# A parametric rectifier on ScalarE carries the sign of the weights through their narrowing, in a kernel of gated recurrent attention and two MLPs on one core

## The chip, the cores and the metric

One core of a Trainium2 chip runs one program. The metric is the time of the program on the device in microseconds; the kernel before has a median of 514.72 us over three runs (514.72, 515.02 and 509.17).

## The reference

Three stages follow one another. The first is a recurrence with gates over 768 steps, for 2 batches and 8 heads of 40 features; the other two are MLPs over the 1,536 resulting tokens of 320 features.

```python
# recurrence, for each batch and head
m_new = maximum(f[t] + m, i[t])
C = exp(f[t] + m - m_new) * C + exp(i[t] - m_new) * outer(v[t], k[t])
n = exp(f[t] + m - m_new) * n + exp(i[t] - m_new) * k[t]
y[t] = sigmoid(o[t]) * (C @ q[t]) / max(abs(n @ q[t]), 1)
# first MLP: w_a, w_b 320 x 1536, w_out 1536 x 320
x = (x @ w_a) * (x @ w_b) @ w_out
# second MLP: w_in 320 x 2048, w_out 2048 x 320
h = x @ w_in
out = (h * sigmoid(h)) @ w_out
```

The weights of both MLPs arrive as 64-bit floats, everything else as 32-bit floats. The products are formed to about 24 bits.

## The kernel before, in words

**Work and tiles.** The recurrence is cut into chunks of 128 tokens. A unit is one chunk of all heads of one batch; the two batches take turns, so there are 12 units. For each unit VectorE scans the decay factors into a matrix (`decays`, L329), TensorE forms scores (L349), VectorE weighs them (`weigh`, L356), TensorE forms values (L362) and the carried state (L372, L382), and VectorE, ScalarE and GpSimd combine the outputs (L418 to L436). `x_transposed` (L448) turns a unit's output by features into a ring `xring` for the first MLP. ScalarE's sigmoid of a unit's output gate is L413.

The MLPs are cut into tiles of 128 hidden features: 12 tiles for the first and 16 for the second. For each tile and each block of two or three units, `first_layer` (L473) forms the hidden products, ScalarE and VectorE form the gate (L506 and L512, or L517 for the second MLP), `split_g` (L486) splits it into a high part (ScalarE, L488) and a rest (GpSimd, L197), and `second_layer` (L482 to L484) adds it into the output.

**Preparation of the weights.** Each weight tile is loaded as 64-bit numbers, seen as pairs of 32-bit words (`raw_j`, L173 and L179, queue of SyncE). `narrowed` (L185) makes 32-bit floats of them, with one ScalarE and three VectorE instructions: ScalarE scales the high word, read as a float, by 2^-111, which moves its exponent field (L188); VectorE shifts the result left by three bits, which puts the exponent and the mantissa where a 32-bit float has them and pushes the sign out (L189); VectorE adds the top three bits of the low word (L190); VectorE adds the sign bit of the high word (L192). ScalarE then rounds the tile to a high part (L206, L214, L217 for the first MLP; L225, L228 for the second) and GpSimd forms the rest (`rest`, L197). A tile of the first MLP is narrowed in two parts, of 448 and 512 columns; a tile of the second in one, of 704 columns. That makes 24 and 16 calls. The parts of the first MLP are loaded into 4 buffers in turn, those of the second into 3; the narrowed tiles lie in 2 buffers each (`cvt`, `cvt2`), which come free when GpSimd has formed the last rest.

**Order.** The list `ORDER` (L31) names the parts of the work up to the last pass of the first MLP; the program is written in that order. A planner (`schedule_with_timeline_sim`, L709) then sets the order of the instructions on each engine: it plays the program with modelled costs and issues what is ready, earlier parts first. So the order on an engine may differ from the list, and it is fixed once the program is built. On each engine instructions then run in that order, and one that waits holds back all behind it. The preparation of the second MLP's tiles (`prep2`, L615) is issued from the last pass of the first MLP on (`block`, L622). 150 small products (`warm`, L296) run on TensorE near the start while it has little else to do.

Of the kernel before, what the change touches and what calls it, by code (L numbers as in the profile page):

```python
# [8 lines left out]
F32 = mybir.dt.float32  # L9
# [3 lines left out]

# The first MLP's passes: a block of tokens and the tiles of the hidden features. The first blocks take
# two passes each, so that the weights' preparation spreads over more products.
PASSES = ((0, range(0, 5)),
# [10 lines left out]

# The order in which the parts of the work are issued up to the last pass of the first MLP, by name:
# l<unit>.* loads of a unit, u<unit>.* its steps, lw<j> and w<j>.* loads and preparation of a weight tile,
# m<pass>.<j>.* products of a pass; those marked ! go ahead of all others that are ready.  # L30
ORDER = """  # L31
# [31 lines left out]

# Parts that wait for the end of another on VectorE.
AFTER = {'w1.a': 'u1.out', 'w1.b': 'u1.out', 'u4.d0': 'u3.w1'}

ACT = mybir.ActivationFunctionType
ALU = mybir.AluOpType
# [3 lines left out]
def tile_mlstm_gated_mlps(ctx: ExitStack, tc: tile.TileContext, i_gate, f_gate, q_cols, k_cols, kvo, w1, w2,  # L72
                          out):
    nc = tc.nc
    B, S, _, H, D = kvo.shape
    BH = B * H
    DM = H * D
    P = 128
    C = 128                      # tokens of a chunk of the recurrence
    NC = S // C  # L80
    NT = B * NC                  # units: a chunk of all heads of a batch; the batches take turns
    DV = D + 1                   # values and the normalizer's column
    G = 3                        # heads of a group; the groups are heads 0-2, 3-5, 5-7
    GR = G * D
    GH = (0, 3, 5)
    SLOT = {h: (h // G, h % G) if h < 6 else (2, h - 5) for h in range(H)}
    BLOCKS = {1: (2, 2, 2, 3, 3), 2: (3, 3, 3, 3)}     # units of each block of the MLPs
    TB = 3 * P
    UNITS, AT = {}, {}
    for m, sizes in BLOCKS.items():  # L90
        for blk, n in enumerate(sizes):
            lo = sum(sizes[:blk])
# [3 lines left out]
    J1, J2 = w1.shape[0], w2.shape[0]  # L96
    KT = DM - 2 * P              # rows of the last tile of the contraction over features
    WN = 10 * P + 2 * DM
    EARLY = 4                    # first units, while the MLPs need little PSUM
    BUSY = 6                     # first units, while VectorE prepares weights  # L100
    WARM = 150                   # matmuls that only keep the clock up
    WS = 2.0 ** 8                # scale of the weights on chip
    NEG = -1e30
    PSUM = bass.MemoryType.PSUM
# [18 lines left out]
    idb = const.tile([P, P], BF16, name="idb")  # L123
    ident8 = cat.tile([P, H, C], F32, name="ident8")
    mask = cat.tile([P, G], F32, name="mask")
    bmask = cat.tile([P, G, G, DV], F32, name="bmask")
    isg = cat.tile([P, NC, 2, BH], F32, name="isg")
    gb = cat.tile([GR, B * G, NC], F32, name="gb")
    fsd = dram.tile([BH, S], F32, name="fsd")
    x1 = {u: const.tile([P, 3 * P], F32, name=f"x1_{u}") for u in range(NT) if AT[1, u][0] < NB1 - 1}  # L130

    def place(u):
        c, b = divmod(u, B)
        return b, c, slice(c * C, (c + 1) * C)

# [1 line left out]
    un = {}  # L137

    def load_q(u):
        b, c, s = place(u)  # L140
        t = at.tile([GR, G, C], F32, tag="qT", name=f"qT_u{u}")
        nc.sync.dma_start(out=t, in_=q_cols[b, c])
        un["q", u] = t

    # Each head's keys by rows of its group, among zeros.
    kz = [cat.tile([GR, G, G, C], F32, name=f"kz{i}") for i in range(2)]

# [12 lines left out]
    def load_fs(u):  # L160
        b, c, s = place(u)
        t = at.tile([P, H, C], F32, tag="e", name=f"e_u{u}")
        nc.sync.dma_start(out=t, in_=fsd[b * H:(b + 1) * H, s].partition_broadcast(P))
# [17 lines left out]

# [1 line left out]
    W = {}  # L183

    def narrowed(r, c):  # L185
        lo32, hi32 = r[:, :, 0], r[:, :, 1]
        cu = c.bitcast(U32)
        nc.scalar.activation(out=c, in_=hi32.bitcast(F32), func=ACT.Copy, scale=2.0 ** -111)  # L188
        nc.vector.tensor_scalar(out=cu, in0=cu, scalar1=3, scalar2=None, op0=ALU.logical_shift_left)  # L189
        nc.vector.scalar_tensor_tensor(out=cu, in0=lo32, scalar=29, in1=cu,  # L190
                                       op0=ALU.logical_shift_right, op1=ALU.bitwise_or)
        nc.vector.scalar_tensor_tensor(out=cu, in0=hi32, scalar=0x80000000, in1=cu,  # L192
                                       op0=ALU.bitwise_and, op1=ALU.bitwise_or)
        return c
# [3 lines left out]

    # First layers: hi hi hi hi [hi_a; lo_a] [lo_b; hi_b] lo lo lo lo; then w_out's hi and lo.
    def split_w1(j, part):  # L200
# [18 lines left out]

    # First layer: hi hi [hi; lo] lo lo; then w_out's hi and lo.  # L220
    def split_w2(j, pool, tag, bufs):
# [9 lines left out]

# [1 line left out]
    scratch = [wp.tile([P, WN], F32, tag="w", name="scratch", bufs=J1) for _ in range(2)]  # L233
# [60 lines left out]

    # Keeps TensorE's clock up while it waits.
    def warm(n):  # L296
# [4 lines left out]

# [1 line left out]
    state = {}  # L303

    def chunk(u):
# [26 lines left out]
        def scale_v():  # L332
            T["v"] = vx = at.tile([P, H, DV], F32, tag="vx", name=f"vx_u{u}")
            nc.gpsimd.tensor_copy(out=vx[:, :, D:DV], in_=isb.unsqueeze(2))
            nc.gpsimd.tensor_tensor(out=vx[:, :, 0:D], in0=un["v", u],
# [22 lines left out]
        def values(n):  # L358
            if n == 0:
                T["y1"] = ps_at.tile([P, H, DV], F32, tag="at", name=f"y1_u{u}")  # L360
            for h in range(4 * n, 4 * n + 4):
# [82 lines left out]

    # A block's tokens by features: hi hi [hi; hi] lo lo [lo; lo]
    px = {}
# [10 lines left out]

# [1 line left out]
    # Slot of the weights, slot of the tokens.  # L459
    PAIRS = {  # L460
# [30 lines left out]

    # The parts of an MLP's work on a block, for the tiles js of the hidden features.
    def mlp(m, blk, js):
# [45 lines left out]

# [1 line left out]
    ch = [chunk(u) for u in range(NT)]  # L541
    run0, expf0, expi0 = gates(0, C)
    run1, expf1, expi1 = gates(C, S)
    passes = [mlp(1, blk, js) for blk, js in PASSES]
# [31 lines left out]
    def load_i():  # L576
        nc.sync.dma_start(out=ig, in_=i_gate.rearrange("b h s -> (b h) s"))

    parts = {"lf": load_f, "li": load_i, "const": constants, "bmask": masks, "zeros": zeros, "sel": selectors,
             "warm": lambda: warm(WARM), "run0": run0, "expf0": expf0, "expi0": expi0, "run1": run1,  # L580
             "expf1": expf1, "expi1": expi1, "starts": gate_starts, "prod": gate_products,
             "pg0": lambda: gate_columns(True), "pg1": lambda: gate_columns(False)}
    for u in range(NT):
        parts.update({f"u{u}.{n}": f for n, f in ch[u].items()})
# [129 lines left out]
```

## Time and profile before

| | |
|---|---|
| Median of three runs | 514.72 us |
| All runs | 514.72, 515.02, 509.17 us |
| Profiled execution: span | 509.0 us (its time outside the span is not shown) |
| TensorE busy | 474.2 us, 93% |
| VectorE busy | 234.7 us, 46% |
| ScalarE busy | 209.9 us, 41% |
| GpSimd busy | 272.7 us, 54% |
| Mean granted TensorE clock | 0.982 |

The span goes from the first to the last instruction of one profiled execution. The shares are averages over stages that differ: VectorE has nearly all of its work in the first 140 us and between 240 and 340 us. In the profile PE is TensorE's products, PEld its weight loads, DVE VectorE, ACT ScalarE, POOL GpSimd and SPq the queue of loads. A group of instructions is shown with its line, engine, operation, tiles and shape, then the count, busy time, mean time of one in ns, and the idle time ahead of them with what ended it.

### The profile page before, as it was taken

To read this page: it belongs to the slowest core of one execution; us is meant where nothing else is said; L and a number is where in the kernel's file an instruction comes from. 1 tells how busy PE (TensorE), PEld (TensorE's weight loads), DVE (VectorE), ACT (ScalarE), POOL (GpSimd) and SP (SyncE) were. 2 spreads that over 40 slices of the span, in tenths; PEclk is the share of its full clock that TensorE was granted. 3 is DMA by queue.
4 is the path that set the end of the run, shared out by engine and by line. 5 is a ranking of instruction groups with operands and counts; after the bars stand their busy time and mean duration, and the time that the engine had idled before them with its cause. 6 is when DMAs were issued, how large, how long until landed. Compare 5 with 4: busy or idle time off the path is not lost.

```text
span 509.0 us, 8482 instructions
## 1 busy us (share of the span) xinstructions
PE 474.2 (93%) x3261; PEld 460.6 (90%) x3261; DVE 234.7 (46%) x368; ACT 209.9 (41%) x479; POOL 272.7 (54%) x305
## 2 busy tenths in 40 slices
PE   7898788897799999999989998999999999999996
PEld 6798778786699999999989987899999999999996
DVE  7999999889934254543674667710010010000000
ACT  4255545544322322222444453663353344334332
POOL 5548987987942241323583788773333433334333
PEclk9988998999989999999999999999999999999999
DMA  7666657636310012104342153100010001001001
GB/s 230 214 196 208 196 174 196 200 123 193 92 57 1 0 54 72 40 1 160 124 135 94 57 169 117 58 1 1 1 39 1 1 0 40 2 0 40 0 1 39
DMA packets 25091, 42.33 MB, mean 83 GB/s; under 512 B 2156, under 2 KB 18348, under 8 KB 25052
## 3 DMA queue, kind: packets, MB, share of 16 engines
q1 hardware_dynamic: 25052, 41.80, 25.9%
q8 instruction: 25, 0.41, 0.3%
q14 instruction: 14, 0.11, 0.1%
HBM read 38.99 MB, written 2.02 MB: 81 GB/s over the span
## 4 chain that ended last, share of the span: by engine, by line
PE 58%; DVE 15%; POOL 14%; ACT 5%; issue 4%; DMA 3%; SPq 0%; ACTq 0%; DVEq 0%; POOLq 0%
PE h L473 31%; POOL w_j L197 9%; PE acc L482 7%; PE acc L483 7%; PE acc L484 7%; DVE e_u L329 4%; DVE cvt_j L190 3%; DVE cvt_j L192 2%; DMA e_u<-fsd 2%; ACT cvt_j L188 2%; PE s_u L349 2%; DVE cvt_j L189 2%; POOL tl_j L197 2%; PE y_u L362 2%; POOL g L197 1%
## 5 line engine op out<-in xcount | busy, mean ns | idle before, releaser
L473 PE MATMUL h<-xring,w_j 128*128 128x384 f32 (+1 forms) x1472 | 264.7, 321 | 8.8 <-DVE g L512 7.3
L473 PEld LDWEIGHTS h<-xring,w_j 128*128 128x128 f32 x1472 | 230.2, 190 | 14.8 <-DVE g L512 11.7
L197 POOL TENSOR_TENSOR g<-g,g 128x384 fp32r<-128x384 f32 (+1 forms) x124 | 121.5, 980 | 180.5 <-ACT g L488 178.7
L482 PE MATMUL acc<-w_j,g 128*128 128x320 f32 x336 | 102.8, 315 | 1.6 <-ACT g L488 1.5
L483 PE MATMUL acc<-w_j,g 128*128 128x320 f32 x336 | 101.4, 310 | 0.0
L488 ACT CAST g<-g 128x384 fp32r<-128x384 f32 (+1 forms) x124 | 59.7, 482 | 98.5 <-DVE g L512 60.0
L197 POOL TENSOR_TENSOR w_j<-cvt_j,w_j 128x320 fp32r<-128x320 f32 (+2 forms) x72 | 79.5, 1104 | 9.8 <-ACT w_j L225 5.0
L484 PE MATMUL acc<-w_j,g 128*128 128x320 f32 x336 | 77.2, 315 | 1.6 <-POOL g L197 1.6
L482 PEld LDWEIGHTS acc<-w_j,g 128*128 128x128 f32 x336 | 63.7, 190 | 3.5 <-ACT g L488 3.4
L483 PEld LDWEIGHTS acc<-w_j,g 128*128 128x128 f32 x336 | 63.8, 190 | 0.0
L484 PEld LDWEIGHTS acc<-w_j,g 128*128 128x128 f32 x336 | 56.8, 189 | 2.7 <-POOL g L197 2.6
L517 ACT ACTIVATE g<-h 128x384 f32<-128x384 f32 x64 | 31.6, 493 | 60.0 <-PE h L473 53.5
L512 DVE TENSOR_TENSOR g<-a,h 128x256 f32<-128x256 f32 (+1 forms) x60 | 27.9, 466 | 49.8 <-PE h L473 49.5
L197 DVE TENSOR_TENSOR xring<-px_u,xring 128x384 fp32r<-128x384 f32 x24 | 12.4, 548 | 83.2 <-PE h L473 80.5
L190 DVE SCALAR_TENSOR_TENSOR cvt_j<-raw_j,cvt_j 128x704 uint32<-128x704 uint32 (+2 forms) x40 | 46.8, 1173 | 0.9
L188 ACT ACTIVATE cvt_j<-raw_j 128x704 f32<-128x704 f32 (+2 forms) x40 | 28.9, 726 | 39.5 <-POOL w_j L197 37.4
L192 DVE SCALAR_TENSOR_TENSOR cvt_j<-raw_j,cvt_j 128x704 uint32<-128x704 uint32 (+2 forms) x40 | 39.4, 986 | 0.6
L506 ACT ACTIVATE a<-h 128x256 f32<-128x256 f32 (+1 forms) x60 | 25.5, 424 | 32.9 <-PE h L473 32.7
L189 DVE TENSOR_SCALAR cvt_j<-cvt_j 128x704 uint32<-128x704 uint32 (+2 forms) x40 | 22.5, 565 | 23.7 <-ACT cvt_j L188 23.7
L349 PE MATMUL s_u<-qT_u,kz 120*128 120x128 f32 x192 | 28.8, 289 | 3.1 <-ACT a L506 2.3
L349 PEld LDWEIGHTS s_u<-qT_u,kz 120*128 120x128 f32 x192 | 25.2, 198 | 3.9 <-ACT a L506 2.5
L362 PE MATMUL y_u<-vx_u,e_u 128*128 128x41 f32 x192 | 26.5, 280 | 2.2 <-DVE e_u L356 2.2
(84 smaller groups left out, 379.0 us busy)
## 6 DMA issues: line engine op xcount, KB each, us to landing
raw_j<-in_w_dram SPq DMA_DIRECT2D x16, 704.0 KB
raw_j<-in_w_dram SPq DMA_DIRECT2D x12, 512.0 KB
kvo_u<-in_kvo_dram SPq DMA_DIRECT2D x12, 480.0 KB
raw_j<-in_w_dram SPq DMA_DIRECT2D x12, 448.0 KB
e_u<-fsd SPq DMA_DIRECT2D x10, 512.0 KB
qT_u<-in_q_cols_dram SPq DMA_DIRECT2D x12, 180.0 KB
kz<-in_k_cols_dram SPq DMA_DIRECT2D x36, 60.0 KB
out_dram<-osb SPq DMA_DIRECT2D x12, 160.0 KB
```

The costliest lines, as they stand in the source:

```text
L188: nc.scalar.activation(out=c, in_=hi32.bitcast(F32), func=ACT.Copy, scale=2.0 ** -111)
L189: nc.vector.tensor_scalar(out=cu, in0=cu, scalar1=3, scalar2=None, op0=ALU.logical_shift_left)
L190: nc.vector.scalar_tensor_tensor(out=cu, in0=lo32, scalar=29, in1=cu, op0=ALU.logical_shift_right, op1=ALU.bitwise_or)
L192: nc.vector.scalar_tensor_tensor(out=cu, in0=hi32, scalar=0x80000000, in1=cu, op0=ALU.bitwise_and, op1=ALU.bitwise_or)
L197: return eng.tensor_tensor(out=out_, in0=x, in1=hi.bitcast(F32), op=ALU.subtract)
L349: nc.tensor.matmul(out=s[:, i], lhsT=kz[u % 2][:, j, g], rhs=un["q", u][:, g], start=True, stop=True)
L362: nc.tensor.matmul(out=T["y1"][:, h], lhsT=un["e", u][:, h], rhs=T["v"][:, h], start=True, stop=True)
L473: nc.tensor.matmul(out=po, lhsT=w[:, wi * P:(wi + 1) * P], rhs=xt[:, :, xi], start=(n == 0), stop=(n == len(pairs) - 1))
L482: nc.tensor.matmul(out=o, lhsT=hi, rhs=w[:, off:off + DM], start=first, stop=False)
L483: nc.tensor.matmul(out=o, lhsT=hi, rhs=w[:, off + DM:off + 2 * DM], start=False, stop=False)
L484: nc.tensor.matmul(out=o, lhsT=lo, rhs=w[:, off:off + DM], start=False, stop=last)
L488: nc.scalar.copy(out=t[:, 0], in_=g)
```

## The change

In `narrowed` the scaling on ScalarE uses the function Prelu in place of Copy: for an input that is not negative the result is the input times 2^-111 as before; for a negative one it is that times alpha, -2^32, so a positive number whose exponent field is higher by 32. The shift by three bits puts that bit of the exponent where the sign belongs. The third VectorE step, which took the sign from the high word, is dropped. The only other edits are comments that are taken out (blank lines stand for most of them; not shown).

```diff
     def narrowed(r, c):
         lo32, hi32 = r[:, :, 0], r[:, :, 1]
         cu = c.bitcast(U32)
-        nc.scalar.activation(out=c, in_=hi32.bitcast(F32), func=ACT.Copy, scale=2.0 ** -111)
+
+        nc.scalar.activation(out=c, in_=hi32.bitcast(F32), func=ACT.Prelu, scale=2.0 ** -111, alpha=-2.0 ** 32)
         nc.vector.tensor_scalar(out=cu, in0=cu, scalar1=3, scalar2=None, op0=ALU.logical_shift_left)
         nc.vector.scalar_tensor_tensor(out=cu, in0=lo32, scalar=29, in1=cu,
                                        op0=ALU.logical_shift_right, op1=ALU.bitwise_or)
-        nc.vector.scalar_tensor_tensor(out=cu, in0=hi32, scalar=0x80000000, in1=cu,
-                                       op0=ALU.bitwise_and, op1=ALU.bitwise_or)
         return c
```

## Rows read from the trace of the kernel before

**Rows 1.** Stretches: busy us (and instructions) per engine, granted clock, DMA.
```profile
core 0: us, PE busy (x) PEld busy (x) DVE busy (x) ACT busy (x) POOL busy (x), PEclk, DMA share, GB/s
0.00:140.00 140.00, 115.35 (x924) 108.30 (x925) 128.43 (x193) 65.94 (x164) 107.26 (x133) 0.95 0.60 184
140.00:240.00 100.00, 99.62 (x750) 99.38 (x750) 41.67 (x97) 26.18 (x64) 32.34 (x42) 0.99 0.14 42
240.00:340.00 100.00, 94.22 (x555) 88.26 (x554) 61.65 (x74) 52.17 (x113) 71.02 (x70) 1.00 0.30 103
340.00:509.00 169.00, 164.98 (x1039) 164.68 (x1037) 2.97 (x6) 65.59 (x139) 62.03 (x61) 1.00 0.04 13
```

**Rows 2.** VectorE by line and shape: count, busy us, mean ns.
```profile
L192 DVE SCALAR_TENSOR_TENSOR cvt_j<-raw_j,cvt_j 128x704 uint32<-128x704 uint32 x16 | 18.5, 1159 | 0.5
...
L190 DVE SCALAR_TENSOR_TENSOR cvt_j<-raw_j,cvt_j 128x512 uint32<-128x512 uint32 x12 | 12.2, 1015 | 0.2
...
L192 DVE SCALAR_TENSOR_TENSOR cvt_j<-raw_j,cvt_j 128x512 uint32<-128x512 uint32 x12 | 10.5, 878 | 0.0
...
L192 DVE SCALAR_TENSOR_TENSOR cvt_j<-raw_j,cvt_j 128x448 uint32<-128x448 uint32 x12 | 10.3, 861 | 0.1
...
L189 DVE TENSOR_SCALAR cvt_j<-cvt_j 128x512 uint32<-128x512 uint32 x12 | 6.5, 539 | 2.1 <-ACT cvt_j L188 2.1
```

**Rows 3.** Chain of waits, first 140 us: share by line.
```profile
by line: DVE e_u L329 14.1%; DVE cvt_j L190 9.4%; DVE cvt_j L192 7.4%; issue 7.3%; POOL tl_j L197 5.7%; POOL w_j L197 5.7%; DVE cvt_j L189 5.4%; DMA e_u<-fsd 4.3%; PE h L473 4.1%; DVE x_u L433 2.9%; ACT cvt_j L188 2.7%; DVE e_u L356 2.4%; D
```

**Rows 4.** Waits, first 140 us: total, times, longest.
```profile
ACT w_j L214 <- DVE cvt_j L192: 21.3, 11, 4.6
...
ACT w_j L206 <- DVE cvt_j L192: 12.4, 6, 3.7
```

**Rows 5.** Waits of the load queue, whole span.
```profile
SPq L173 <- DVE cvt_j L192: 35.7, 16, 5.1
```

**Rows 6.** GpSimd, one form: first 140 us, then 140 to 240.
```profile
L197 POOL TENSOR_TENSOR g<-g,g 128x256 fp32r<-128x256 f32 x14 | 15.0, 1074 | 1.7 <-ACT g L488 1.7
...
L197 POOL TENSOR_TENSOR g<-g,g 128x256 fp32r<-128x256 f32 x22 | 16.2, 738 | 40.2 <-ACT g L488 40.2
```

**Rows 7.** Chain of waits, 240 to 340 us.
```profile
by line: POOL w_j L197 40.3%; PE h L473 16.0%; issue 8.1%; POOL g L197 6.1%; ACT cvt_j L188 5.8%; ACT w_j L225 4.5%; ACT g L488 3.4%; PE acc L482 2.8%; PE acc L484 2.6%; PE acc L483 2.5%; PE px_u L452 1.6%; DVE cvt_j L192 1.6%; ACT L517 1.3
```

**Rows 8.** Timeline, two tiles of that stretch: start, us, idle before.
```profile
297.73 0.85 ACT L188 ACTIVATE cvt_j<-raw_j 128x704 f32<-128x704 f32 x1 [2.65 <-POOL w_j L197]
...
298.48 0.50 ACT L488 CAST g<-g 128x384 fp32r<-128x384 f32 x1
...
299.06 1.02 POOL L197 TENSOR_TENSOR g<-g,g 128x384 fp32r<-128x384 f32 x1 [1.36 <-ACT g L488]
...
300.03 3.40 POOL L197 TENSOR_TENSOR w_j<-cvt_j,w_j 128x256 fp32r<-128x256 f32 x3
...
300.85 1.31 DVE L192 SCALAR_TENSOR_TENSOR cvt_j<-raw_j,cvt_j 128x704 uint32<-128x704 uint32 x1
...
302.09 0.54 DVE L512 TENSOR_TENSOR g<-a,h 128x384 f32<-128x384 f32 x1
...
308.11 0.84 ACT L188 ACTIVATE cvt_j<-raw_j 128x704 f32<-128x704 f32 x1 [2.64 <-POOL w_j L197]
```

**Rows 9.** ScalarE by line and shape.
```profile
L188 ACT ACTIVATE cvt_j<-raw_j 128x704 f32<-128x704 f32 x16 | 13.6, 847 | 23.1 <-POOL w_j L197 23.1
...
L228 ACT CAST w_j<-cvt_j 128x320 fp32r<-128x320 f32 x16 | 7.3, 459 | 0.0
...
L413 ACT ACTIVATE kvo_u<-kvo_u 128x320 f32<-128x320 f32 x12 | 5.5, 466 | 3.3 <-DMA kvo_u<-in_kvo_dram 3.3
...
L413 ACT ACT_TABLE_LOAD x1 | 1.3, 1283 | 0.0
```

**Rows 10.** ScalarE timeline, 0 to 140 us: first, last of eight sigmoid groups.
```profile
11.69 0.83 ACT L413 ACTIVATE kvo_u<-kvo_u 128x320 f32<-128x320 f32 x2
...
138.26 0.47 ACT L413 ACTIVATE kvo_u<-kvo_u 128x320 f32<-128x320 f32 x1
```

## The prediction

> **What bounds the kernel now.** I read the stretches first, because shares over the whole span mix stages [rows 1]. In the first 140 us VectorE is busy for 128.4 us (92%) and TensorE for 115.4, of which some belongs to products that only fill time; GpSimd has 107.3, ScalarE 65.9. So VectorE is the fullest engine there, and TensorE is idle for 24.6 us. From 140 to 240 us TensorE is busy for 99.6 of 100: nothing else matters. From 240 to 340 us it is idle for 5.8 us, and it also does fewer instructions than it could (555 in 100 us; the last stretch has 1039 in 169 us, which is 615 in 100): about 60 instructions, or 10 us, are lost. After 340 us TensorE alone sets the pace and VectorE has 3 us of work. The change touches VectorE and ScalarE, so it can move the end only through the first and the third stretch. In both, what they finish earlier passes on to the end, since TensorE is full behind them.
>
> The chain of waits of the first 140 us comes next [rows 3]: the dropped line L192 has 7.4% of it, 10.4 us. The waits say who is held up by it: ScalarE's rounding of a narrowed tile waits on L192 for 21.3 and 12.4 us there [rows 4]. Then the third stretch: in its chain GpSimd's rests have 40.3%, L192 1.6% [rows 7].
>
> **The sum, part by part.**
>
> *The dropped step, first stretch.* Of the 24 calls for the first MLP, 12 have 448 columns at 861 ns and 12 have 512 at 878 ns [rows 2]: 10.3 + 10.5 = 20.8 us leave VectorE's 128.4. From above, the gain is all 20.8 us: VectorE would stay as full as it is and the stretch would end that much earlier. From below it is nothing, if another engine takes over at once. Between them stands the chain's share, 10.4 us [rows 3]. I take 10.4: VectorE at 108 of 130 us would then be 83% full, and the 24.6 us in which TensorE is idle [rows 1] have room for it, while a gain of 20.8 would ask TensorE to work in 119 us with hardly an idle moment, although each unit's steps wait for each other.
>
> *What it gives to GpSimd.* One form, the rest of the gate at 128x256, takes 1074 ns in the first 140 us and 738 ns in the next stretch, where VectorE is 42% busy [rows 6]: 46% more beside a full VectorE. GpSimd's rests on the chain are 5.7 + 5.7% [rows 3], 16 us; of their 46%, some 5 us lie in the chain as slowing, and L192 is 16% of VectorE's busy time (20.8 of 128.4) but more of what reads two tensors. I take 1.4 us, with ends 0 and 5.
>
> *The dropped step, third stretch.* 16 x 1159 ns = 18.5 us leave VectorE [rows 2]. The loop that sets the pace is another one [rows 8]: ScalarE's L188 waits for GpSimd's rest to free a buffer, L488 stands behind it in ScalarE's order, GpSimd idles 1.36 us for L488, then forms the gate's rest (1.02) and three weight rests (3.40). VectorE's steps run beside these 3.40 us. L192 only delays VectorE's L512 behind it (302.09), and so a L488 whose result GpSimd could not take before 303.4 anyway. So I cost it at nothing, with GpSimd's rests as the cover. If the cover is gone (a new order in which L488 goes ahead of L188 each time), about 1 us of that idle goes for each of some six pairs of tiles: 6 us, the upper end. The lower end is 0.
>
> *Prelu for Copy.* The trace has no Prelu. Its nearest rows say that ScalarE's time goes by size and hardly by function: a sigmoid of 128x320 takes 466 ns and a rounding copy of that size 459 [rows 9]. So L188 stays at 847 ns for 704 columns. Bounds: nothing from below, since the instruction reads and writes the same; from above a second pass, another 847 ns.
>
> *The load queue.* No load is added or moved, but L192 was the last reader of a raw buffer. The loads L173 wait on it for 35.7 us in all [rows 5], and what is queued behind them (units' inputs, the scans' factors) waits too. With L190 as the last reader each buffer comes free some 0.9 us earlier (861 and 878 ns). I add nothing: weights that come earlier also compete with the units' loads, and the loads are not the bound.
>
> Sum: 10.4 + 1.4 = 11.8 us. The profiled execution has a span of 509.0 us; what lies around it is not shown, and the fastest of the three runs, 509.17, stands as close to it as a run can. Its own time less the sum is 497.2 us. The median of the runs is 5.7 us longer than the span; taken from it, the same sum gives 514.7 - 11.8 = **502.9 us**, 2.3% less. That is the forecast, **503 us**.
>
> **A rule that bears on the second term.** The row above shows GpSimd slower beside a full VectorE, with no cause in it [rows 6]. The Trainium skill's GPSIMD Engine Reference, section Key points, says that GpSimd shares its SBUF interfaces with VectorE and contends with VectorE instructions that have two SBUF inputs, which L192 has. By that rule most of the slowing, not a share of it, would come from steps like L190 and L192, and the sum would be near 15 us and not 11.8.
>
> **The rivals.**
>
> *All of it counts* (0.15). VectorE is the bound of the first stretch throughout, so 20.8 us go: 493.9. For it speaks 92% busy; against it that the chain runs on VectorE for about half of its length only.
>
> *The next queue takes over* (0.25). GpSimd at 107.3 us and the units' own chain bind as soon as VectorE eases. Then only the part of TensorE's idle time goes that is L192's share of VectorE's work: 16% of 24.6 = 3.9 us, 510.8. For it speaks that GpSimd's rests are on the chain too [rows 3].
>
> *Prelu costs more than Copy* (0.03). L188 stands in the third stretch's loop: about 12 of its 16 tiles x 0.85 us = 10.2 us there, against 11.8 gained: 513.1.
>
> *Prelu needs another function table* (0.04). The trace loads a table three times, 1283 ns each [rows 9]. Ten sigmoids stand in eight groups between narrowings in the first 140 us [rows 10]; if the two functions did not share a table, 1 + 6 x 2 + 1 loads would come there and one before the third stretch: 15 x 1.283 = 19.2 us on ScalarE, which has 74 us of idle time in that stretch. All on the path would give 522.1; half of it 512.5. The Trainium skill's page ScalarE: Activation LUTs, section Table sets, names relu, copy, identity and abs as functions that every table has, and not the parametric rectifier; with the drain that the page adds to a load (2.66 us in all, an estimate from that page: 40 us) the time would be 543. No run so far shows a Prelu or that drain.
>
> *Slower: the planner's new order* (0.08). With cheaper narrowings the planner may put them ahead of the units' steps on VectorE. Each narrowing put ahead holds a unit back by L189 and L190, 0.54 + 1.02 = 1.56 us for 512 columns [rows 2]. Eight units are scanned from stored factors in that stretch; two narrowings ahead of each cost 8 x 3.1 = 25 us, and TensorE waits for the units' outputs: 514.7 - 11.8 + 25 = 528. It decides from some 22 us on, 14 narrowings put ahead; below that the result stays within 2%. Against it: the list is unchanged, and the units' parts stand early in it.
>
> **Numbers.** The forecast has 0.45, with a range of its own of 499 to 507. I take 2% for what a measurement can tell from no change: below 504.4 or above 525.0. Faster is three quarters of the forecast's chance and all of the first rival: 0.49. Slower is the last rival and a part of the table's: 0.10. The rest, 0.41, is within 2%. The range goes from the first rival, 494, up to 514, where the next queue has taken all; outside lie the slower cases and a gain that adds the third stretch's 6 us to 20.8.
>
> **What would show it.** VectorE's busy time falls by 39 us in all. Right: VectorE's full stretch ends near 128 us, not 140, TensorE's idle time ahead of it falls by about as much, and the third stretch keeps its pace of 10.4 us for two tiles (297.73 to 308.11 [rows 8]). L188 at 847 ns and three table loads show Prelu to be free; more loads show the table's rival. If the first stretch is as long as before with VectorE near 80%, the next queue has it; if L329 or L356 come later than before, the order has changed. A third stretch that is shorter by more than 2 us means that the cover was not what I took it for.

## The result and the profile after

The changed kernel takes 494.21 us (median of four runs, 493.73 to 496.84); the kernel before, beside it on the same chip, 514.29 us (509.17 to 515.02). The ratio is 0.9651 [0.9594, 0.9708]: **faster by 3.5%**. The profiled execution took 493.73 us with a span of 491.8, against the 509.0 of before: 17.2 us of the difference can be followed in the two traces.

In the changed file the narrowing is Prelu L189, shift L190, low word L191; every later line has a number smaller by one (L512 is L511, GpSimd's rest L197 is L196). The stretches after, with the columns of [rows 1] (busy us and instructions of TensorE, its weight loads, VectorE, ScalarE, GpSimd; granted clock; DMA):

```profile
core 0: us, PE busy (x) PEld busy (x) DVE busy (x) ACT busy (x) POOL busy (x), PEclk, DMA share, GB/s
0.00:140.00 140.00, 123.04 (x995) 118.54 (x996) 113.76 (x174) 69.21 (x175) 108.95 (x140) 0.94 0.61 185
140.00:240.00 100.00, 100.00 (x750) 99.90 (x749) 44.64 (x98) 29.00 (x65) 32.27 (x41) 1.00 0.19 58
240.00:340.00 100.00, 98.09 (x592) 95.14 (x591) 38.45 (x50) 53.12 (x115) 65.25 (x71) 1.00 0.25 85
340.00:491.80 151.80, 147.54 (x930) 147.24 (x928) 2.97 (x6) 59.30 (x125) 55.00 (x55) 1.00 0.04 14
```

Against [rows 1]: in the first 140 us VectorE falls from 128.4 to 113.8 us and TensorE rises from 115.4 to 123.0, at much the same granted clock (0.94 after 0.95). GpSimd does 140 instructions there and not 133, in 109.0 us. In the third stretch TensorE rises from 94.2 to 98.1 us and from 555 to 592 instructions. So both stretches gained, and the prediction had given the third nothing.

Fixed windows cut different work, so I set two landmarks on ScalarE: its first narrowing of a 704-column tile (the second MLP's weights begin) and its last table load (they are done). Start, duration, engine, line; the kernel before and then the changed one:

```profile
243.29 0.83 ACT L188 ACTIVATE cvt_j<-raw_j 128x704 f32<-128x704 f32 x1
...
330.88 1.28 ACT L517 ACT_TABLE_LOAD   x1
```

```profile
232.26 0.83 ACT L189 ACTIVATE cvt_j<-raw_j 128x704 f32<-128x704 f32 x1
...
313.20 1.28 ACT L516 ACT_TABLE_LOAD   x1
```

Up to the first landmark 243.29 - 232.26 = 11.0 us are gained. Between the two it is 87.59 before and 80.94 after, another 6.65. From the second to the end it is 178.1 and 178.6, a loss of 0.5. These add up to the 17.2 us.

VectorE's lines after (count, busy us, mean ns, idle before):

```profile
L191 DVE SCALAR_TENSOR_TENSOR cvt_j<-raw_j,cvt_j 128x704 uint32<-128x704 uint32 x16 | 21.9, 1370 | 0.5
...
L190 DVE TENSOR_SCALAR cvt_j<-cvt_j 128x704 uint32<-128x704 uint32 x16 | 9.9, 618 | 23.5 <-ACT cvt_j L189 23.5
```

The step L192 is gone with its 39.4 us (16 + 12 + 12 calls). VectorE's busy time on the page falls from 234.7 to 199.8, by 34.9 only, because neighbouring records overlap a little: the lines add up to 251.4 us before and 212.8 after, and some of that overlap goes with the step. The 704-column shift L190 takes 618 ns a call, where it took 524; the low word's step beside it takes 1370 for 1429, so the two together change little.

The chain of waits of the first 130 us after, by line:

```profile
by line: PE h L472 11.7%; issue 8.3%; DVE e_u L328 6.3%; DMA raw_j<-in_w_dram 5.8%; PE s_u L348 5.7%; DVE cvt_j L191 4.7%; DVE cvt_j L190 4.2%; DMA e_u<-fsd 3.9%; POOL tl_j L196 3.5%; POOL w_j L196 3.3%; PE y_u L361 2.7%; DMA fsd<-scratch 2
```

In [rows 3] the narrowing's three VectorE lines had 22.2% of 140 us; its two now have 8.9% of 130. TensorE's L472, the first layer's products, leads the chain with 11.7%. ScalarE's rows:

```profile
L189 ACT ACTIVATE cvt_j<-raw_j 128x704 f32<-128x704 f32 x16 | 13.6, 849 | 16.6 <-POOL w_j L196 16.6
...
L516 ACT ACT_TABLE_LOAD x1 | 1.3, 1283 | 0.0
```

Prelu takes 849 ns where Copy took 847 [rows 9], and loads of a table at the narrowings there are none: the program still has three. The loop of the third stretch, two tiles of it (start, us, idle before and its releaser):

```profile
297.03 0.84 ACT L189 ACTIVATE cvt_j<-raw_j 128x704 f32<-128x704 f32 x1 [2.12 <-POOL w_j L196]
...
298.34 1.02 POOL L196 TENSOR_TENSOR g<-g,g 128x384 fp32r<-128x384 f32 x1 [1.35 <-ACT g L487]
...
299.31 2.88 POOL L196 TENSOR_TENSOR w_j<-cvt_j,w_j 128x256 fp32r<-128x256 f32 x3
...
303.57 2.75 POOL L196 TENSOR_TENSOR w_j<-cvt_j,w_j 128x256 fp32r<-128x256 f32 x3 [0.39 <-ACT w_j L224]
...
306.36 0.83 ACT L189 ACTIVATE cvt_j<-raw_j 128x704 f32<-128x704 f32 x1 [2.12 <-POOL w_j L196]
```

Two tiles take 306.36 - 297.03 = 9.33 us; in [rows 8] it is 10.38. The order is the same, and GpSimd's two idle gaps too, 1.35 and 0.39 us. What has shrunk is GpSimd's own work: the three weight rests take 2.88 and 2.75 us in place of 3.40 and 3.28. By form (count, busy us, mean ns), before (250 to 330 us) and then after (235 to 313 us), the parts between the landmarks where the rests run:

```profile
L197 POOL TENSOR_TENSOR w_j<-cvt_j,w_j 128x320 fp32r<-128x320 f32 x14 | 15.9, 1135 | 1.1
L197 POOL TENSOR_TENSOR w_j<-cvt_j,w_j 64x128 fp32r<-64x128 f32 x14 | 13.3, 952 | 1.1
L197 POOL TENSOR_TENSOR w_j<-cvt_j,w_j 128x256 fp32r<-128x256 f32 x13 | 12.8, 988 | 3.6 <-ACT w_j L225 3.6
```

```profile
L196 POOL TENSOR_TENSOR w_j<-cvt_j,w_j 128x256 fp32r<-128x256 f32 x15 | 15.1, 1007 | 2.1 <-ACT w_j L224 1.9
L196 POOL TENSOR_TENSOR w_j<-cvt_j,w_j 128x320 fp32r<-128x320 f32 x14 | 12.4, 887 | 1.1
L196 POOL TENSOR_TENSOR w_j<-cvt_j,w_j 64x128 fp32r<-64x128 f32 x14 | 10.2, 726 | 1.1
```

The 128x256 rest, which comes first and runs beside the low word's step in both kernels (298.46 to 300.11 in the changed one), takes 988 and 1007 ns. The two behind it, which ran beside L192, fall from 952 to 726 and from 1135 to 887: 0.47 us a tile, and 14 tiles make 6.6 of the 6.65 us.

### The profile page after: what moved, and what is told of

The parts are those of the page before. It is cut to its first block, busy times and chain, and to the rows that moved or that the text cites. A ratio compares the mean times of both kernels' runs of the same rounds, so it can differ in the third digit from the quotient of the medians.

```text
span 491.8 us, 8440 instructions
## 1 busy us (share of the span) xinstructions
PE 468.7 (95%) x3261; PEld 460.8 (94%) x3261; DVE 199.8 (41%) x328; ACT 210.6 (43%) x479; POOL 261.5 (53%) x305
## 4 chain that ended last, share of the span: by engine, by line
PE 67%; POOL 11%; DVE 8%; DMA 4%; issue 4%; ACT 4%; SPq 1%; ACTq 0%; POOLq 0%; DVEq 0%
PE h L472 35%; PE acc L481 8%; PE acc L483 8%; PE acc L482 8%; POOL w_j L196 7%; PE s_u L348 3%; PE y_u L361 2%; ACT cvt_j L189 2%; POOL g L196 2%; DVE e_u L328 2%; DMA raw_j<-in_w_dram 2%; DVE cvt_j L191 1%; DVE cvt_j L190 1%; PE px_u L451 1%; PE y_u L371 1%
## 5 line engine op out<-in xcount | busy, mean ns | idle before, releaser
L472 PE MATMUL h<-xring,w_j 128*128 128x384 f32 (+1 forms) x1472 | 260.3, 319 | 6.6 <-DVE g L511 4.2
L472 PEld LDWEIGHTS h<-xring,w_j 128*128 128x128 f32 x1472 | 229.9, 190 | 9.1 <-DVE g L511 5.1
L196 POOL TENSOR_TENSOR g<-g,g 128x384 fp32r<-128x384 f32 (+1 forms) x124 | 119.1, 961 | 185.5 <-ACT g L487 184.5
L196 POOL TENSOR_TENSOR w_j<-cvt_j,w_j 128x320 fp32r<-128x320 f32 (+2 forms) x72 | 69.7, 969 | 6.5 <-ACT w_j L224 3.0
L511 DVE TENSOR_TENSOR g<-a,h 128x256 f32<-128x256 f32 (+1 forms) x60 | 28.1, 468 | 54.0 <-PE h L472 53.7
L196 DVE TENSOR_TENSOR xring<-px_u,xring 128x384 fp32r<-128x384 f32 x24 | 12.4, 548 | 85.6 <-PE h L472 82.0
L191 DVE SCALAR_TENSOR_TENSOR cvt_j<-raw_j,cvt_j 128x704 uint32<-128x704 uint32 (+2 forms) x40 | 44.7, 1118 | 0.9
L189 ACT ACTIVATE cvt_j<-raw_j 128x704 f32<-128x704 f32 (+2 forms) x40 | 28.9, 725 | 28.5 <-POOL w_j L196 27.0
L190 DVE TENSOR_SCALAR cvt_j<-cvt_j 128x704 uint32<-128x704 uint32 (+2 forms) x40 | 24.9, 627 | 30.1 <-ACT cvt_j L189 30.1
L348 PE MATMUL s_u<-qT_u,kz 120*128 120x128 f32 x192 | 30.9, 304 | 0.6 <-DVE y_u L419 0.6
L348 PEld LDWEIGHTS s_u<-qT_u,kz 120*128 120x128 f32 x192 | 27.4, 213 | 0.8 <-DVE y_u L419 0.8
L361 PEld LDWEIGHTS y_u<-vx_u,e_u 128*128 128x128 f32 x192 | 25.5, 197 | 1.7 <-DVE e_u L355 1.5
```

What stands on the lines that cost most here:

```text
L196: return eng.tensor_tensor(out=out_, in0=x, in1=hi.bitcast(F32), op=ALU.subtract)
L348: nc.tensor.matmul(out=s[:, i], lhsT=kz[u % 2][:, j, g], rhs=un["q", u][:, g], start=True, stop=True)
L361: nc.tensor.matmul(out=T["y1"][:, h], lhsT=un["e", u][:, h], rhs=T["v"][:, h], start=True, stop=True)
L472: nc.tensor.matmul(out=po, lhsT=w[:, wi * P:(wi + 1) * P], rhs=xt[:, :, xi], start=(n == 0), stop=(n == len(pairs) - 1))
```

## Experiments

In each kernel below the edit is shown against the changed kernel, except where it says otherwise. The theory after the result: the first stretch gains what the chain gave L192, and the third gains because L192, a step with two SBUF inputs, slowed GpSimd's rests beside it. The rivals: Prelu itself does something; the third stretch gains by VectorE's time or by ScalarE's order; all of it is one gain of VectorE's.

**1. Prelu, with the step kept.**

```diff
+        nc.vector.scalar_tensor_tensor(out=cu, in0=hi32, scalar=0x80000000, in1=cu,
+                                       op0=ALU.bitwise_and, op1=ALU.bitwise_or)
```

> Prelu in place of Copy, and the third VectorE step kept as well. If Prelu costs what Copy does and the whole gain comes from the dropped step, the time is that of the kernel before (ratio 0.99 to 1.01, L188 at 847 ns for 704 columns, three table loads, third stretch at 10.4 us for two tiles). If Prelu itself brings something (a shorter wait behind it, another clock), the ratio is below 0.99. If Prelu costs more and the dropped step hid that, it is above 1.01.

511.51 us, ratio 0.9983 [0.9943, 1.0022]. Its landmarks:

```profile
247.16 0.83 ACT L188 ACTIVATE cvt_j<-raw_j 128x704 f32<-128x704 f32 x1
...
334.74 1.28 ACT L517 ACT_TABLE_LOAD   x1
```

87.58 us lie between them, as before. Prelu in place of Copy is worth nothing within that interval; the gain comes with the dropped step.

**2 and 3. The change for one MLP's weights only.**

```diff
+        if m == 1:      # in the other kernel: m == 2
             nc.scalar.activation(... func=ACT.Prelu, scale=2.0 ** -111, alpha=-2.0 ** 32)
+        else:
+            nc.scalar.activation(... func=ACT.Copy, scale=2.0 ** -111)
...
+        if m == 2:      # in the other kernel: m == 1; the sign step as before
```

> The change for the tiles of the first MLP alone (24 of 40 narrowings); those of the second are narrowed as before. If the first stretch gave 12 us and the third stretch 5 to 6, this kernel gains 11 to 14 us (ratio 0.973 to 0.979) and its third stretch keeps 10.4 us for two tiles with GpSimd's three rests at 3.3 to 3.4 us. If the whole gain came from the first stretch, it gains 17 to 20 us (ratio about 0.965).

> The change for the tiles of the second MLP alone (16 of 40). If the third stretch gave 5 to 6 us, this kernel gains that much (ratio 0.988 to 0.991), two tiles take 9.3 us and the three rests 2.8 to 2.9 us. If the third stretch gains only when the first one has changed the order or the time at which it begins, the ratio is 0.995 to 1.005.

The first MLP's tiles alone: 0.9832 [0.9760, 0.9904], 8.6 us, less than the 11 to 14 expected, though the interval reaches 12.3. The second's alone: 0.9848 [0.9796, 0.9900], 7.8 us, where 5 to 6 were expected. Landmarks of the first kernel, then of the second:

```profile
237.05 0.83 ACT L191 ACTIVATE cvt_j<-raw_j 128x704 f32<-128x704 f32 x1
...
324.64 1.28 ACT L521 ACT_TABLE_LOAD   x1
```

```profile
243.87 0.83 ACT L189 ACTIVATE cvt_j<-raw_j 128x704 f32<-128x704 f32 x1
...
324.75 1.28 ACT L521 ACT_TABLE_LOAD   x1
```

The first has 87.59 us between them, as before; the second 80.88, as the whole change. Each part gains in its own stretch alone.

**4. The change again, beside these.** No edit.

> The whole change on the same chip as the other three: ratio 0.959 to 0.971 as measured. The gains of the two parts alone should add up to this one within 3 us if they are independent; if they share a cause, their sum misses it by more.

495.61 us, 0.9658 [0.9601, 0.9716]. The parts, 1.7% and 1.5%, add up to the whole's 3.4% within the intervals. Its profiled span is 497.0 us, where the same program had 491.8; its first stretch shows a difference:

```profile
0.00:140.00 140.00, 123.82 (x953) 119.84 (x954) 112.08 (x172) 67.92 (x172) 103.21 (x136) 0.89 0.59 184
```

The granted clock is 0.89 here and was 0.94. Its first landmark stands at 237.51, 5.25 us later than in the first execution, so the whole difference lies ahead of it, and 80.87 us between the landmarks are the same. First landmarks are to be compared at equal clocks: from kernel 1 (0.89, 247.16) to this one (0.89) the gain is 9.65 us, from before (0.95) to the change (0.94) 11.0. Even so they scatter. Up to this landmark TensorE's order is the same in before and kernels 1, 3 and 11 (243.29, 247.16, 243.87 and 241.63 us, mean 244.0), and again in the change and kernels 4, 2, 5, 6, 9 and 12 (232.26, 237.51, 237.05, 235.04, 240.82, 234.93 and 232.68 us, mean 235.8). The difference of the means is 8.2 us.

**5 and 6. What slows GpSimd.** The change, with a useless VectorE step in each of the second MLP's 16 tiles, for whose result nobody waits: in kernel 5 one of two SBUF inputs, in kernel 6 one of one input.

```diff
+        if m == 2:   # kernel 5
+            nc.vector.scalar_tensor_tensor(out=lo32.bitcast(F32), in0=c, scalar=1.0, in1=c,
+                                           op0=ALU.mult, op1=ALU.max)
+        if m == 2:   # kernel 6
+            nc.vector.tensor_reduce(out=r[:, 0:1, 0].bitcast(F32), in_=c, op=ALU.max,
+                                    axis=mybir.AxisListType.X)
```

> The whole change, and for each tile of the second MLP one more VectorE instruction with two SBUF inputs of 704 columns (the narrowed tile against itself, written over the low words that are no longer needed); nothing waits for its result. If the third stretch gained because GpSimd's rests no longer run beside that step, the three rests go back to 3.3 to 3.4 us, two tiles to about 10.4 us, and 5 to 7 us of the gain are lost (ratio to before 0.976 to 0.981). If it gained because ScalarE waited for the step, nothing is lost (0.963 to 0.969, rests at 2.8 to 2.9 us).

> As the one before, but the added VectorE instruction reads one SBUF input and writes one column (a maximum over 704 columns). VectorE is as full and its order as long as with the two-input one. If two SBUF inputs are what slows GpSimd, the rests stay at 2.8 to 2.9 us, two tiles take 9.3 us and the ratio to before stays at 0.963 to 0.969. If VectorE's time or its order is what counts, as much is lost as with the two-input one (0.976 to 0.981).

Kernel 5: 0.9802 [0.9740, 0.9865], so about 7 of the change's 17.5 us are lost; 87.86 us lie between the landmarks. Kernel 6: 0.9659 [0.9538, 0.9780], an interval too wide to exclude a loss of 6 us by itself; but between the landmarks it has 80.61 us, where the change has 80.94, so nothing is lost there (granted clock 1.00 in the third stretch of both). The added steps, kernel 5 and then 6:

```profile
L193 DVE SCALAR_TENSOR_TENSOR raw_j<-cvt_j 128x704 f32<-128x704 f32 x16 | 18.8, 1177 | 0.5
```

```profile
L193 DVE TENSOR_REDUCE raw_j<-cvt_j 128x1 f32<-128x704 f32 x16 | 14.2, 885 | 0.5
```

And GpSimd's three rests of two neighbouring tiles, in the same order:

```profile
297.10 3.40 POOL L198 TENSOR_TENSOR w_j<-cvt_j,w_j 128x256 fp32r<-128x256 f32 x3
...
301.85 3.28 POOL L198 TENSOR_TENSOR w_j<-cvt_j,w_j 128x256 fp32r<-128x256 f32 x3 [0.37 <-ACT w_j L226]
```

```profile
298.24 2.87 POOL L197 TENSOR_TENSOR w_j<-cvt_j,w_j 128x256 fp32r<-128x256 f32 x3
...
302.48 2.76 POOL L197 TENSOR_TENSOR w_j<-cvt_j,w_j 128x256 fp32r<-128x256 f32 x3 [0.39 <-ACT w_j L225]
```

With the two-input step they are back at 3.40 and 3.28, the values of before to a hundredth; with 14.2 us of one-input VectorE work added they stay at 2.87 and 2.76. So neither VectorE's time nor ScalarE's wait on it counts in this loop; a step of the dropped one's kind does, by GpSimd. The two dummies also differ in what they write (704 columns against one); the runs do not separate that from the second input.

**7 and 8. The same two dummies in the first MLP's 24 narrowings** (`m == 1`).

> The whole change, and for each of the 24 narrowings of the first MLP one more VectorE instruction with one SBUF input (a maximum over the 448 or 512 columns); nothing waits for its result. If the first stretch is bound by VectorE's time, some 12 to 15 us of work come back and most of the 10 us gained there are lost (ratio 0.980 to 0.988). If what counted was that the rounding on ScalarE no longer waits for the step, less than 3 us are lost (0.966 to 0.972).

> As the one before, with a two-input instruction of the same columns. VectorE's time alone gives about the same loss as the one-input form (within 3 us). If the first stretch also gained from GpSimd's freedom, the loss is 2 to 5 us larger, and GpSimd's 128x512 rests take 1.5 to 1.6 us and not 1.36.

The one-input step, 24 calls, 15.4 us: 0.9713 [0.9622, 0.9804]. That is 2.8 us by the ratios, whose intervals overlap with the change's; the profiled executions, both at a granted clock of 0.94 in the first 140 us, say 238.96 - 232.26 = 6.7 us at the first landmark, and 4 us against the latest of the change's landmarks at a like clock (235.04). The two-input step, 22.0 us: 0.9949 [0.9911, 0.9987], about 15 us lost. The first 140 us of the one, then of the other:

```profile
0.00:140.00 140.00, 119.54 (x958) 114.06 (x959) 119.81 (x197) 68.51 (x172) 107.93 (x139) 0.94 0.59 184
```

```profile
0.00:140.00 140.00, 117.66 (x873) 112.50 (x874) 123.98 (x187) 65.04 (x161) 110.10 (x131) 0.85 0.58 176
```

GpSimd's 128x512 rest of the first MLP's weights in that stretch, before, after, and in kernel 8 (count, busy us, mean ns):

```profile
L197 POOL TENSOR_TENSOR w_j<-cvt_j,w_j 128x512 fp32r<-128x512 f32 x11 | 17.8, 1618 | 1.5 <-DMA w_j<-tl_j 1.2
```

```profile
L196 POOL TENSOR_TENSOR w_j<-cvt_j,w_j 128x512 fp32r<-128x512 f32 x12 | 16.3, 1355 | 0.0
```

```profile
L198 POOL TENSOR_TENSOR w_j<-cvt_j,w_j 128x512 fp32r<-128x512 f32 x12 | 18.7, 1556 | 1.6 <-ACT w_j L207 1.6
```

A single form also moves with what it happens to meet: in kernel 7, beside the one-input step, it takes 1481 ns. So the sum of a tile's four rests says more (mean ns of each form in the first 140 us):

| | 128x512 | 64x128, twice | 128x320 | sum of the four |
|---|---|---|---|---|
| before | 1618 | 864 | 975 | 4321 |
| the change | 1355 | 834 | 992 | 4015 |
| kernel 7, one input | 1481 | 718 | 1044 | 3961 |
| kernel 8, two inputs | 1556 | 771 | 1172 | 4270 |

Here too the two-input step slows GpSimd, by about 0.3 us a tile, and the one-input step does not. So the 4 to 6.7 us of kernel 7 are not seen in GpSimd's rests: in this stretch VectorE's time counts in part, at most 6.7 of 15.4 us. TensorE's order in kernels 7 and 8, the same in both, differs from the change's, and what that is worth is not told apart.

Kernel 8 loses more than the 8.6 us that kernel 2 gained. Part of it is TensorE's clock. From 120 to 130 us TensorE is busy throughout, but at the lower of its two clock levels for nearly all of that time:

```profile
120.00:130.00 10.00, 10.00 (x49) 10.00 (x49) 5.71 (x12) 2.05 (x5) 5.39 (x8) 0.52 0.30 84
```

That is 49 products where the change does 84 there at a clock of 1.00: 35 products of 0.12 us, some 4 us (an estimate). Nor is it one execution's chance: in all ten of kernel 8 the granted clock over the span is 0.959 to 0.972, in ten of the change 0.969 to 0.986. Why the clock is lower with this step stays open.

**9 to 11. Less work for GpSimd.** If its rests set the pace, moving the smallest of each second-MLP tile to VectorE should help. Kernel 9 does so after the change; 10 moves the first MLP's 64x128 rests as well; 11 makes kernel 9's edit on the kernel before.

```diff
-        rest(nc.gpsimd, t[KT:P, 2 * P:3 * P], c[KT:P, 2 * P:3 * P], t[KT:P, 2 * P:3 * P])
+        rest(nc.vector, t[KT:P, 2 * P:3 * P], c[KT:P, 2 * P:3 * P], t[KT:P, 2 * P:3 * P])
...
-            rest(nc.gpsimd, tl[p], c[p, 0:P], t[p, s_])     # kernel 10 only
+            rest(nc.vector, tl[p], c[p, 0:P], t[p, s_])
```

> The whole change, and the rest of 64 rows x 128 columns in each tile of the second MLP is formed on VectorE and not on GpSimd (0.72 us each there). If GpSimd's time still sets the third stretch's pace, two tiles take 7.9 to 8.4 us instead of 9.3, near TensorE's own 8.1 for two tiles, and 5 to 8 us go beyond the change (ratio to before 0.950 to 0.956). If the pace is set by the chain through ScalarE, little goes (0.963 to 0.967). If the added two-input VectorE step slows the other rests as much as it saves, nothing goes.

> As the one before, and also the two rests of 64 rows x 128 columns in each tile of the first MLP on VectorE (24 x 0.83 us on GpSimd). With the dropped step gone VectorE has room in the first stretch, but every two-input step on it slows GpSimd: between 3 us better than the kernel with the second MLP's rests alone and 4 us worse. Faster means that GpSimd was the next queue in the first stretch; slower means that VectorE still is the fullest.

> The kernel before, without the change, with the rest of 64 x 128 in each tile of the second MLP on VectorE. If GpSimd's time sets the third stretch there as well, two tiles go from 10.4 to 9.2 to 9.6 us and 5 to 8 us are gained (ratio 0.984 to 0.990). If VectorE, with the sign step still on it, cannot take the work, nothing or less is gained (0.995 to 1.01).

Kernel 9: 0.9668 [0.9603, 0.9733], no gain over the change and not the 5 to 8 us expected. Kernel 11: 0.9963 [0.9914, 1.0013], none over before. Kernel 10: 505.42 us (498.61 to 508.76) beside 511.77, without an interval, and each of its runs is longer than any of kernel 9's (493.82 to 496.54), which goes with VectorE as the fullest engine of the first stretch; how much worse stays open. In kernel 11 two tiles still take 10.38 us (290.62 to 301.00): GpSimd idles 1.90 and 1.44 us ahead of the gate's rests, where it idled 1.36 us ahead of one of the two. Where kernel 9's gain went, in one tile:

```profile
290.97 0.84 ACT L188 ACTIVATE cvt_j<-raw_j 128x704 f32<-128x704 f32 x1 [2.27 <-POOL w_j L195]
291.71 0.50 ACT L486 CAST g<-g 128x384 fp32r<-128x384 f32 x1
...
292.36 1.02 POOL L195 TENSOR_TENSOR g<-g,g 128x384 fp32r<-128x384 f32 x1 [1.42 <-ACT g L486]
...
293.34 2.28 POOL L195 TENSOR_TENSOR w_j<-cvt_j,w_j 128x256 fp32r<-128x256 f32 x2
```

The rests are down to 2.28 us, but ScalarE's narrowing now stands ahead of the rounding of the gates in every tile, not in every second one, and GpSimd idles 1.42 us each time. A tile takes 4.68 us; it was 9.33 for two. What GpSimd saved it waits for.

**12. A third buffer for the narrowed tile** (and one raw tile fewer, for room), so that ScalarE's narrowing need not wait for GpSimd's rest.

```diff
-  ... tag="raw2", ... bufs=3)      ... tag="cvt2", ... bufs=2)
+  ... tag="raw2", ... bufs=2)      ... tag="cvt2", ... bufs=3)
```

> The whole change, with three buffers and not two for the narrowed tiles of the second MLP (and two, not three, for its raw tiles, to make room). ScalarE's L189 then no longer waits for the rest that GpSimd has just formed, and the rounding of the gate behind it is not held up. If that round trip through the buffer is what is left of GpSimd's idle time in the third stretch, its gaps of 1.35 us go, two tiles take 7.8 to 8.5 us instead of 9.3, near TensorE's 8.1, and 4 to 6 us go beyond the change (ratio to before 0.953 to 0.960). If TensorE or VectorE holds the pace there, nothing goes (0.963 to 0.969).

493.53 us, 0.9666 [0.9616, 0.9716], the same as the change. Its loop:

```profile
288.39 0.83 ACT L189 ACTIVATE cvt_j<-raw_j 128x704 f32<-128x704 f32 x1 [2.12 <-POOL w_j L196]
289.12 0.50 ACT L487 CAST g<-g 128x384 fp32r<-128x384 f32 x1
...
289.70 1.02 POOL L196 TENSOR_TENSOR g<-g,g 128x384 fp32r<-128x384 f32 x1 [1.34 <-ACT g L487]
...
290.68 2.87 POOL L196 TENSOR_TENSOR w_j<-cvt_j,w_j 128x256 fp32r<-128x256 f32 x3
```

The planner only issues the narrowing one tile further ahead, so it still waits 2.12 us for a rest, and the gap of 1.34 us is still there. No version here is clearly faster than the change.

## Why the prediction was right and wrong

**The sign and the first stretch: right, but by another way.** The terms 10.4 + 1.4 = 11.8 us stand against 9.65 and 11.0 in two pairs of traces at the first landmark, 8.2 on the mean of eleven, and kernel 2's 8.6 [4.9, 12.3] over the whole time. The chain's share was the better choice between 0 and 20.8. But the prediction had VectorE's full stretch end 12 us earlier, near 128 us. From 120 to 140 us, before and then after:

```profile
120.00:140.00 20.00, 14.05 (x104) 12.52 (x103) 19.83 (x27) 6.83 (x17) 16.92 (x18) 0.99 0.35 104
120.00:140.00 20.00, 20.00 (x165) 19.99 (x164) 8.78 (x16) 6.06 (x18) 11.25 (x16) 1.00 0.25 72
```

VectorE, full there before, is busy for 8.78 of 20 us; its full stretch now ends near 119 us. So about the whole 20.8 us came free on VectorE, and only half of it reached the landmark, because TensorE has no idle time left from 120 us on. That the chain's share of the old trace gave that half is in part luck.

**The third stretch: the step that failed.** The prediction costed the dropped step there at nothing, "with GpSimd's rests as the cover", and expected 10.4 us for two tiles to stay. The measured term is 6.65 us. It was not that the cover was outlasted: the cover shrank. Before, the rests ran for 3.40 us beside L192, and without it for 2.88; kernel 5 brings the 3.40 back and kernel 6 does not. The prediction took the row's 3.40 as a fixed duration, though it had put a price on just this contention one part earlier, for the first stretch. Its upper end of 6 us is near the 6.65 by chance, since it was for another order on ScalarE, which did not come: gaps of 1.35 and 0.39 us as before. The prediction's own last sign, a third stretch shorter by more than 2 us, is the one that came true. With 6.65 added its sum would have been 18.4, and against the median 496.3.

**The rule.** The Trainium skill's GPSIMD Engine Reference, section Key points, has GpSimd contend with VectorE instructions of two SBUF inputs. The runs agree: 3.40 us with such a step more, 2.87 with a one-input step (kernels 5 and 6). The prediction applied it to the first stretch alone, where it would have made the sum 15; it bore on the third as well. The Trainium skill's page SBUF — State Buffer, section SBUF: two separate sides, has whichever of the two starts first hold the shared ports for its whole instruction, while the other stands still. The trace of the kernel before agrees, and shows that both engines pay:

```profile
245.47 0.89 DVE L190 SCALAR_TENSOR_TENSOR cvt_j<-raw_j,cvt_j 128x704 uint32<-128x704 uint32 x1
245.63 1.61 POOL L197 TENSOR_TENSOR g<-g,g 128x384 fp32r<-128x384 f32 x1 [3.85 <-ACT g L488]
...
269.06 0.89 DVE L192 SCALAR_TENSOR_TENSOR cvt_j<-raw_j,cvt_j 128x704 uint32<-128x704 uint32 x1
...
279.33 2.23 POOL L197 TENSOR_TENSOR w_j<-cvt_j,w_j 128x256 fp32r<-128x256 f32 x3
...
299.17 1.65 DVE L190 SCALAR_TENSOR_TENSOR cvt_j<-raw_j,cvt_j 128x704 uint32<-128x704 uint32 x1
```

At 245.47 L190 starts first and keeps its 0.89 us, and the gate's rest takes 1.61; at 299.06 the gate's rest starts first and keeps its 1.02 [rows 8], and L190 takes 1.65. L192 takes 0.89 us with GpSimd idle (269.06) and 1.31 beside the rests [rows 8]. The three rests take 2.23 us with VectorE idle (279.33), 2.75 and 2.88 beside the low word's step alone, 3.28 and 3.40 beside both steps. So the step that is left still costs them 0.5 to 0.65 us a tile.

**The median.** The forecast of 503 us, with its own range of 499 to 507, was missed; 494.2 lies only just inside the wider range, 494 to 514, and that it does is luck, since the lower end came from a rival that fell. The sum was taken from the median, 514.7. The spans of the two profiled executions differ by 17.2 us and the medians by 20.1. The prediction put the profiled 509.0 beside the run of 509.17; but all runs listed with their span take 1.7 to 2.4 us more than it, so that execution took near 511 us (an estimate from these). It lies some 3 us below its median and the change's 0.5 below its own, which is where the remaining 2.9 us come from. Beside the experiments, over 11 to 13 runs each, the kernel before has medians of 511.46 to 512.55 us, so 514.3 was on the long side, and the 17.5 us of experiment 4 is the better size of the gain.

**The rivals.** *All of it counts* gave 493.9, and the time is 494.2, but by another way: kernel 2 shows 8.6 us from the first MLP's tiles and not 20.8, and much of the rest comes from a stretch which that rival left alone. *The next queue takes over* gave 510.8 and falls, though TensorE's products lead the chain now. *Prelu costs more* and *another table* fall by 849 ns, three table loads and kernel 1's 0.9983; the Trainium skill's page ScalarE: Activation LUTs, section Table sets, leaves the parametric rectifier out of the functions that every table has, and in this case it cost no load. *The planner's new order* came in part, without its loss: all 24 narrowings of the first MLP stand ahead of VectorE's eleventh scan of `decays`, where 21 did, and TensorE's order differs from about its 167th product on. What the new order is worth beside the time that came free was not tested.

**The load queue** was costed at nothing. Its waits on the narrowing's last reader, 35.7 us at L173 [rows 5], are 25.0 after, and no run tells apart what this is worth.

## What to carry to other kernels

When a step with two SBUF inputs leaves VectorE, price it twice: by its share of the chain, and by what GpSimd's work beside it took longer; a stretch that GpSimd paces can gain by the second alone. Before an edit is costed at nothing, ask whether the duration of its cover depends on the edit, by comparing the same form in a stretch without it. To see why a stretch gained, a useless step of like length but another kind is a sharper test than undoing the edit.

## What the runs showed of the hardware

A step with two SBUF inputs on VectorE cost a GpSimd subtraction of 64x128 31% (952 against 726 ns) and one of 128x320 28% (1135 against 887); a one-input reduction in the same place cost them nothing (724 and 873 ns in kernel 6, from 285 to 310 us). VectorE pays too: the step of 704 columns took 0.89 us with GpSimd idle, 1.04 and 1.31 beside its rests.

A one-input step, the 704-column shift, became slower on average (524 to 618 ns) although VectorE has less to do; in the steady loop it takes 0.53 us in both kernels, and the longer calls of the changed one stand ahead of the loop (1.26, 0.71 and 1.06 us from 235 to 243 us). All three overlap work that GpSimd had already begun (at 234.59, 236.17 and 241.53 us). So a step of one input need not be free beside GpSimd, as the reduction was; no run tests this one by itself.

The same program's span differed by 5.2 us between two executions, all of it in the part up to the first landmark, where the granted clock was 0.94 in one and 0.89 in the other (before and kernel 1, with the same order on TensorE: 509.0 at 0.95, 512.8 at 0.89). A gain of 1% in such a stretch needs many executions, or several traces at the same clock.
